# A fused attention and feed-forward kernel on one core: the first attention two steps ahead, matmuls on zeros in TensorE's waits, and batch 2 loaded ahead of two weights

## The chip, the core and the metric

The kernel runs on one core of one Trainium2 chip. The metric is the time of one execution on the device, in microseconds (us). Five engines work beside each other, each through its own list of instructions in order: TensorE (PE, matrix products and transposes), VectorE (DVE), ScalarE (ACT), GpSimd (POOL), and SyncE (SP), which here only issues transfers. POOL and SP start the transfers (DMA), and 16 DMA engines carry them out. TensorE reads SBUF and writes PSUM, from which DVE or ACT copy.

## The reference

Attention over 8 batches, 8 heads, 576 positions, 64 features a head, with 16 extra keys ("beacon") that every position sees, and after it a feed-forward part over the 4608 x 512 result:

```python
k_all = concat([beacon_k, k]); v_all = concat([beacon_v, v])
scores = q @ k_all.T / sqrt(64)           # causal over the 576, the 16 are always seen
a = softmax(scores);  attn = a @ v_all    # per batch and head
x = attn as [4608, 512]
out = ((x @ w1) * (x @ w2)) @ w3 @ w_out  # w1, w2: 512x1024, w3: 1024x1024, w_out: 1024x512
```

## The kernel before

All arithmetic of TensorE is in fp16 with sums in fp32. The work has two streams, which the program's text weaves together by hand: every engine does its instructions in the order in which the Python code issues them.

**Attention.** It goes in steps `s`, eight to a batch (`NSB`): step `s` is one half of the work for one pair of heads, `t`, of batch `b = s // 8`. `scores(s)` (L351) makes the transposed scores of the two heads in two PSUM tiles `ps`, of which there are two in all: eight matmuls in an even step, fourteen in an odd one. `exps(s, j)` (L360, ACT) writes exp of tile `j` to `pT` in SBUF and frees it. `mask(s, j)` (L372, DVE) zeroes what a position must not see. `values(s)` (L389) multiplies by the values, 6 matmuls in an even step and 24 in an odd one, into the only `psV` tile, and DVE divides by the sums into `x16` (L397, L398). The values carry a column of ones, so the sums come with them.

Scores need q and k with the features on the partitions. For batches 0 and 1 they are loaded in fp32 by SP (`load_pair`, L139), cast by DVE (`cast_pair`, L158), transposed on PE (`pe_transpose_pair`, L172) and copied out of PSUM by DVE or ACT (L178). From batch 2 on POOL's transfers load them and cast them to fp16 (`load_q`, L104, `load_k`, L113), and SP issues ten DMA transposes a batch (`transpose_qk`, L128, L129). There are two buffers for a batch's q, k and values, so batch 2 goes where batch 0 was. The last 64 rows of the fifth block of q and k are zeroed once (L481, L482).

**Feed-forward.** `emit_ff(n)` issues the next `n` matmuls of a generator, `stream()`: for blocks of 512 tokens, `ff_ab` (L279) makes (x w1) times (x w2), with ACT (L290) and DVE (L292) behind it, and `ff_out` (L300) multiplies by `Wt` and SP stores the result. `Wt` is w3 times w_out, made once by `fuse()` (L248, L257) behind the first two blocks; for this the eight pieces of w3 lie in the half of `xT` that is free so long, and w_out in `wo16`. Thirty feed-forward matmuls stand between the transposes of batch 1's q and k, 34 in steps 8 to 15, and from step 16 on about 12 in each step. x is turned into `xT` on PE for batches 0 and 1 (`pe_transpose_x`, L188), later by DMA.

**Order of the transfers.** POOL issues, one behind the other: values of batch 0, w1 and w2 (8 pieces), values of batch 1, w_out (4), w3 (8), and from step 3 on q and k of batch 2, values of batch 2, q and k of batch 3, and so on. The weights are 256 KB a piece in fp16 and are read in fp32.

The first attention is steps 0 to 7. Before the main loop stand casts and transposes of the four pairs of batch 0, with `scores(0)` and its exponentials between; in the loop each step issues the scores of the next one, and then its own values.

Of the kernel before, what the change touches and what calls it, by code (L numbers as in the profile page):

```python
# [8 lines left out]
FP32 = mybir.dt.float32  # L9
# [30 lines left out]
def kernel(  # L40
# [81 lines left out]
    def load_v(b, jt):  # L122
        load_kv(b, jt, v, beacon_v, vas[b % NB2][:, jt, :, 0:64])
# [26 lines left out]
    def cast_pair(b, t):  # L150
        if t == 0:
            b16 = bkp.tile([Nb, DM], FP16, name="b16")
            nc.vector.tensor_copy(b16, early_b[b].rearrange("p h d -> p (h d)"))
            early_b[b] = b16
        o16s[t] = []
        for i in range(2):
            o16 = tiny.tile([P, RUN, P], FP16, name=f"o16_{i}")
            nc.vector.tensor_copy(  # L158
                o16[:NR].rearrange("p j (h d) -> p h j d", h=2),
                early_qk[b, t, i][:NR].rearrange("p h (j d) -> p h j d", j=RUN),  # L160
            )
            o16s[t].append(o16)

    def pe_transpose_pair(b, t):
        qT, kT = qTs[b % NB2], kTs[b % NB2]
        for o16, dst, off, copy in (
            (o16s[t][0], qT, 0, nc.vector.tensor_copy if b or t == 0 else nc.scalar.copy),
            (o16s[t][1], kT, Nb, nc.scalar.copy),
        ):
            pt = psM.tile([P, 1024], FP16, name="pm")  # L170
            for j in range(RUN):
                nc.tensor.transpose(pt[:, ds(j * NR, NR)], o16[:NR, j, :], ident[:NR, :NR])  # L172
            if off:
                nc.tensor.transpose(
                    pt[:, ds(S, Nb)], early_b[b][:, ts(t, P)], ident[:Nb, :Nb]
                )
                copy(dst[:, t, 0:Nb], pt[:, ds(S, Nb)])
            copy(  # L178
                dst[:, t, ds(off, S)].rearrange("p (i j) -> p i j", j=RUN),
                pt[:, 0:S].rearrange("p (j i) -> p i j", j=RUN),  # L180
            )

    def pe_transpose_x(b):
        for i in range(NJT):
            pt = psM.tile([P, NT, P], FP16, name="pm")
            n = QTN[i]
            for t in range(NT):
                nc.tensor.transpose(  # L188
                    pt[:, t, 0:n], x16s[b][:n, i, ts(t, P)], ident[:n, :n]
                )  # L190
            dst = xT[:, :, ds(b * S + QT0[i], n)]
            if i % 2:
                nc.scalar.copy(dst, pt[:, :, 0:n])
            else:
                nc.vector.tensor_copy(dst, pt[:, :, 0:n])  # L195

    nc.vector.memset(ident, 1.0)
    nc.vector.memset(MA, 1.0)
# [35 lines left out]
        )  # L234
    for c in range(NJT):
        load_v(0, c)
    for c in range(4):
        for i, w in enumerate((moe_w1, moe_w2)):
            nc.gpsimd.dma_start(
                w12[:, :, ds(i * DF + c * 256, 256)],  # L240
                w[:, ts(c, 256)].rearrange("(t p) f -> p t f", p=P),
            )
# [85 lines left out]
    def emit_ff(n):  # L328
        nonlocal emitted
        for _ in range(n):  # L330
            try:
                next(ff)
            except StopIteration:
                return
            emitted += 1
# [4 lines left out]
    def scores(s):  # L340
        b, t, half = s // (2 * NT), (s // 2) % NT, s % 2
        if half == 0:
            pTs[s // 2] = ptp.tile([P, 2, PW], FP16, name="pT")
        qT, kT = qTs[b % NB2], kTs[b % NB2]
        pss[s] = []
        for g in (2 * half, 2 * half + 1):
            ps = psS.tile([P, 2, 512], FP32, name="ps")
            pss[s].append(ps)
            for jt, q0, n, col in GROUPS[g]:
                for hh in range(2):  # L350
                    nc.tensor.matmul(  # L351
                        ps[:, hh, ds(col, n)],
                        kT[ds(hh * 64, 64), t, ts(jt, P)],
                        qT[ds(hh * 64, 64), t, ds(q0, n)],
                    )

    def exps(s, j):
        g = 2 * (s % 2) + j
        pT = pTs[s // 2]
        nc.scalar.activation(  # L360
            pT[:, :, ds(GO[g], GW[g])], pss[s][j][:, :, 0 : GW[g]], AF.Exp, scale=scale
        )
# [59 lines left out]
    for s in range(2 * NSB, NS):  # L422
        fill[s] = rest * (s - 2 * NSB + 1) // n - rest * (s - 2 * NSB) // n

    cast_pair(0, 0)
    pe_transpose_pair(0, 0)
    cast_pair(0, 1)
    scores(0)
    for j in range(2):
        exps(0, j)  # L430
    pe_transpose_pair(0, 1)
    cast_pair(0, 2)
    for j in range(2):
        mask(0, j)
    pe_transpose_pair(0, 2)
    cast_pair(0, 3)
    pe_transpose_pair(0, 3)
    constants(1)
    for c in range(NJT):
        load_v(1, c)  # L440
    wo_v = moe_w_out.rearrange("(a c p) n -> a p c n", p=P, c=2)
    for a in range(4):
        nc.gpsimd.dma_start(wo16[:, ds(2 * a, 2), :], wo_v[a])
# [1 line left out]
    w316 = xT[:, :, ds(M // 2, 2 * DF)].rearrange("p a (c r) -> p a c r", c=2)  # L445
    for kt in range(NFT):
        nc.gpsimd.dma_start(w316[:, kt // 2, kt % 2], moe_w3[ts(kt, P), :])
    for s in range(NS):
        b, r = s // NSB, s % NSB
        if s == NSB - 1:  # L450
            values(s)
            pe_transpose_x(0)
            cast_pair(1, 0)
            for t in range(NT):
                emit_ff(n_first // NT)
                pe_transpose_pair(1, t)
                if t + 1 < NT:
                    cast_pair(1, t + 1)
            emit_ff(n_first - emitted)
            scores(s + 1)  # L460
            for j in range(2):
                exps(s + 1, j)
                mask(s + 1, j)
            continue
        if s + 1 < NS:
            scores(s + 1)
            exps(s + 1, 0)
        values(s)
        k1 = min(8, fill[s])
        emit_ff(k1)  # L470
        if s + 1 < NS:
            exps(s + 1, 1)
            mask(s + 1, 0)
        emit_ff(fill[s] - k1)
        if s + 1 < NS:
            mask(s + 1, 1)
        if s == 3:
            for t in range(NT):
                load_pair(1, t)
            for i in range(NB2):  # L480
                nc.vector.memset(k16s[i][64:128, 4, :], 0.0)  # L481
                nc.vector.memset(q16s[i][64:128, 4, :], 0.0)  # L482
            for c in range(NJT):
                load_q(2, c)
                load_k(2, c)
        if s == 2 * NSB - 1:
            pe_transpose_x(1)
        if 1 <= b < B - 1:
            if r == 0:
                for c in range(NJT):  # L490
                    load_v(b + 1, c)
                for c in range(NJT if b + 2 < B else 0):
                    load_q(b + 2, c)
                    load_k(b + 2, c)
            if 1 <= r <= NJT:
                transpose_qk(b + 1, r - 1)
# [31 lines left out]
```

## Time and profile before

| | us |
|---|---|
| median of three timed runs | 331.8 (330.7 to 332.42) |
| profiled execution, its own time | 331.28 |
| its span in the trace | 329.6 |
| PE busy | 296.8 (90%) |
| DVE, ACT, POOL busy | 165.4, 160.1, 107.2 |
| mean granted clock of TensorE | 0.979 of full speed |

The span runs from the first to the last instruction; the time of the execution holds some 1.7 us around it. A busy share is a mean over stages that differ. A line of the timeline gives start, duration, engine, source line, operation, output and input, their shapes and, behind an x, the number of instructions drawn together; in brackets stands the idle time ahead of the first one and what ended it. [...]

### The profile page before, as it was taken

What the parts mean: (1) busy time and instruction counts of PE and PEld (TensorE: products, weight loads), DVE (VectorE), ACT (ScalarE), POOL (GpSimd) and SP (SyncE); (2) the same over time, 40 slices, a digit from 0 to 9 for tenths busy, and PEclk for the clock granted to TensorE, in tenths of its full rate; (3) what the DMA queues carried; (4) which work ended last, traced back from release to release, by engine and by line L of the source; (5) the groups of instructions that cost most, each with busy time, mean ns of one, the idle gap of its engine ahead of it and who ended that gap; (6) DMA issues with size and microseconds to landing.
All of it is one profiled execution on the core that took longest, in us unless ns stands there. A gap on an engine that the chain in (4) does not pass through costs nothing.

```text
span 329.6 us, 6963 instructions
## 1 busy us (share of the span) xinstructions
PE 296.8 (90%) x2800; PEld 155.2 (47%) x2800; DVE 165.4 (50%) x392; ACT 160.1 (49%) x232; POOL 107.2 (33%) x143
## 2 busy tenths in 40 slices
PE   1687878727998999999999999999999999999995
PEld 1465544405444554555544555445554544444442
DVE  4546665523555544556565555555564644334442
ACT  1775366723664555356746663664666332130320
POOL 8565147757733385047408611400000000000000
PEclk9999998976999999999999999999999999999999
DMA  8999999999999299979999999991550340301103
GB/s 179 203 196 202 254 220 184 122 145 157 152 136 118 38 127 155 216 134 154 157 148 191 166 146 174 158 133 50 152 57 2 105 96 0 127 2 64 64 2 127
DMA packets 156960, 42.97 MB, mean 130 GB/s; under 512 B 143104, under 2 KB 151296, under 8 KB 156928
## 3 DMA queue, kind: packets, MB, share of 16 engines
q0 software_dynamic: 102240, 17.28, 75.2%
q1 hardware_dynamic: 54688, 25.25, 41.9%
q8 instruction: 22, 0.36, 0.4%
q14 instruction: 10, 0.08, 0.1%
HBM read 39.32 MB, written 9.44 MB: 148 GB/s over the span
## 4 chain that ended last, share of the span: by engine, by line
PE 76%; DMA 9%; ACT 5%; SPq 4%; DVE 3%; issue 1%; DVEq 0%
PE pm L279 33%; PE pm L300 19%; PE pv L389 10%; PE ps L351 8%; DMA st<-in_k_dram 7%; PE pm L257 4%; ACT pT L360 3%; DMA qT<-q 3%; ACT a_sb L290 1%; SPq L129 1%; SPq L128 1%; SPq L139 1%; PE pm L248 1%; DVE gT L292 1%; DVE o L158 1%
## 5 line engine op out<-in xcount | busy, mean ns | idle before, releaser
L279 PE MATMUL pm<-xT,w 128*128 128x512 f16 x576 | 134.3, 383 | 0.7 <-DVE xT L195 0.5
L360 ACT ACTIVATE pT<-ps 128x736 f16<-128x736 f32 (+3 forms) x128 | 106.2, 863 | 45.8 <-PE ps L351 45.3
L290 ACT ACTIVATE a_sb<-pm 128x512 f32<-128x512 f32 x72 | 43.0, 597 | 87.4 <-PE pm L279 86.4
L279 PEld LDWEIGHTS <-w 128*128 128x128 f16 x576 | 53.9, 98 | 60.5 <-issue 2.7
L292 DVE TENSOR_TENSOR gT<-pm,a_sb 128x512 f16<-128x512 f32 x72 | 49.7, 690 | 44.6 <-PE pm L279 44.2
L300 PE MATMUL pm<-Wt,gT 128*128 128x512 f16 x288 | 65.9, 379 | 0.0
L351 PE MATMUL ps<-qT,kT 64*128 64x80 f16 (+3 forms) x704 | 40.5, 243 | 14.6 <-ACT pT L360 6.0
L113 POOL DMA_DIRECT2D va<-in_v_dram x40 | 35.0, 886 | 56.7 <-PE pv L389 37.6
L389 PE MATMUL pv<-va,pT 128*128 128x65 f16 x960 | 45.2, 202 | 3.0 <-DVE x L398 1.3
L397 DVE RECIPROCAL rd<-pv 128x4 f32<-128x4 f32 x64 | 12.1, 189 | 69.9 <-PE pv L389 69.8
L389 PEld LDWEIGHTS <-pT 128*128 128x128 f16 x960 | 36.4, 102 | 14.1 <-DVE pT L372 4.3
L351 PEld LDWEIGHTS <-kT 64*128 64x128 f16 x704 | 22.3, 99 | 42.8 <-issue 31.5
L300 PEld LDWEIGHTS <-gT 128*128 128x128 f16 x288 | 27.1, 98 | 30.4
L310 DVE TENSOR_SCALAR ot<-pm 128x512 f32<-128x512 f32 x36 | 24.9, 691 | 26.0 <-PE pm L300 25.9
L398 DVE TENSOR_TENSOR x<-pv,rd 128x256 f16<-128x256 f32 x64 | 31.4, 491 | 2.3
L104 POOL DMA_DIRECT2D q<-in_q_dram x30 | 25.6, 855 | 15.9 <-DMA va<-in_v_dram 8.0
L113 POOL DMA_DIRECT2D k<-in_k_dram x30 | 25.3, 845 | 10.6 <-DMA va<-in_v_dram 7.0
L372 DVE TENSOR_TENSOR pT<-pT,MB 128x512 f16<-128x512 f16 x64 | 19.4, 324 | 0.0
L257 PE MATMUL pm<-wo,wT 128*128 128x512 f16 x64 | 16.4, 380 | 1.0 <-DVE wT L250 1.0
L172 PE MATMUL pm<-ident,o 96*128 96x96 f16 x96 | 7.8, 242 | 9.3 <-DVE o L158 8.7
L372 DVE TENSOR_TENSOR pT<-pT,MA 128x480 f16<-128x480 f16 x32 | 12.8, 399 | 1.5 <-ACT pT L360 1.5
L172 PEld LDWEIGHTS <-o 96*128 96x128 f16 x96 | 6.2, 116 | 11.6 <-DVE o L158 9.6
(40 smaller groups left out, 87.7 us busy)
## 6 DMA issues: line engine op xcount, KB each, us to landing
out_dram<-ot SPq DMA_DIRECT2D x36, 256.0 KB, 2.4
va<-in_v_dram POOLq DMA_DIRECT2D x24, 128.0 KB, 8.7
q<-in_q_dram POOLq DMA_DIRECT2D x24, 128.0 KB, 9.0
st<-in_q_dram SPq DMA_DIRECT2D x8, 288.0 KB, 7.9
st<-in_k_dram SPq DMA_DIRECT2D x8, 288.0 KB, 8.8
k<-in_k_dram POOLq DMA_DIRECT2D x18, 128.0 KB, 7.8
w<-in_moe_w_dram POOLq DMA_DIRECT2D x8, 256.0 KB, 9.8
xT<-in_moe_w_dram POOLq DMA_DIRECT2D x8, 256.0 KB, 9.8
```

Of the source, the lines that this page charges most:

```text
L104: nc.gpsimd.dma_start(q16s[b % NB2][:rows, c, :].rearrange("s (h d) -> s h d", h=H), q[b, :, ds(c * P, rows), :].rearrange("h s d -> s h d"),)
L113: nc.gpsimd.dma_start(dst[ds(p0, rows)], src[b, :, ds(s0, rows), :].rearrange("h s d -> s h d"))
L257: nc.tensor.matmul(pm, wT[:, rt, :], wo16[:, rt, :], start=(rt == 0), stop=(rt == NFT - 1),)
L279: nc.tensor.matmul(pm, w12[:, kt, ds(i * DF + kf * P, P)], xT[:, kt, ds(mc * 512, 512)], start=(kt == 0), stop=(kt == NKT - 1),)
L290: nc.scalar.activation(a_sb, pm, AF.Copy, scale=GS)
L292: nc.vector.tensor_tensor(gT[:, kf, :], pm, a_sb, ALU.mult)
L300: nc.tensor.matmul(pm, gT[:, kf, ts(mt, P)], Wt[:, kf, :], start=(kf == 0), stop=(kf == NFT - 1),)
L351: nc.tensor.matmul(ps[:, hh, ds(col, n)], kT[ds(hh * 64, 64), t, ts(jt, P)], qT[ds(hh * 64, 64), t, ds(q0, n)],)
L360: nc.scalar.activation(pT[:, :, ds(GO[g], GW[g])], pss[s][j][:, :, 0 : GW[g]], AF.Exp, scale=scale)
L372: nc.vector.tensor_tensor(blk, blk, m.unsqueeze(1).to_broadcast([P, 2, n]), ALU.mult)
L389: nc.tensor.matmul(pv[:, 2 * n + hh, 0:65], pT[:, hh, ds(col, P)], va[:, jt, 2 * t + hh, 0:65], start=(jn == 0), stop=(jn == len(BLK[i]) - 1),
L398: nc.vector.tensor_tensor(x16[:, ds(tiles[0], ni), ds(t * P, P)].rearrange("p i (h d) -> p i h d", h=2), pv[:, 0 : 2 * ni, 0:64].rearrange ...
```

## The change

Four things are changed; the arithmetic of the output stays.

1. `spin(n)` issues `n` matmuls of zeros by zeros into a PSUM tile of the feed-forward pool that nobody reads: ten ahead of everything, two ahead of `scores(0)`, two ahead of `scores(1)`, two ahead of each of the eight `values(s)` of batch 0, and two ahead of the transposes of x: 32 in all. The tile `zeros` is zeroed by DVE first of all.
2. Batch 0 has a loop of its own, in which `ahead(s + 2)` (scores and exponentials) and then `values(s)` are issued. `ahead(1)` stands between the transposes of the second and the third pair. The copies of the third and fourth q out of PSUM go from ACT to DVE. The casts of batch 1's first pair stand ahead of the transposes of x, and its loads come at step 1 in place of step 3.
3. POOL issues q, k and values of batch 2 ahead of w_out and w3.
4. The pad rows of q and k are zeroed by POOL, ahead of w1 and w2, in place of DVE at step 3.

```diff
-            (o16s[t][0], qT, 0, nc.vector.tensor_copy if b or t == 0 else nc.scalar.copy),
+            (o16s[t][0], qT, 0, nc.vector.tensor_copy if b or t != 1 else nc.scalar.copy),
...
+    zeros = const.tile([P, 512], FP16, name="zeros")
+    nc.vector.memset(zeros, 0.0)
+
+    def spin(n):
+        pm = psM.tile([P, 512], FP32, name="pm")
+        for _ in range(n):
+            nc.tensor.matmul(pm, zeros[:, 0:P], zeros)
...
     for c in range(NJT):
         load_v(0, c)
+    for i in range(NB2):
+        nc.gpsimd.memset(k16s[i][64:128, 4, :], 0.0)
+        nc.gpsimd.memset(q16s[i][64:128, 4, :], 0.0)
...
+    def ahead(s):
+        scores(s)
+        for j in range(2):
+            exps(s, j)
+
+    def masks(s):
+        for j in range(2):
+            mask(s, j)
+
+    spin(10)
     cast_pair(0, 0)
     pe_transpose_pair(0, 0)
     cast_pair(0, 1)
-    scores(0)
-    for j in range(2):
-        exps(0, j)
+    spin(2)
+    ahead(0)
     pe_transpose_pair(0, 1)
     cast_pair(0, 2)
-    for j in range(2):
-        mask(0, j)
+    masks(0)
+    spin(2)
+    ahead(1)
     pe_transpose_pair(0, 2)
     cast_pair(0, 3)
+    masks(1)
     pe_transpose_pair(0, 3)
     constants(1)
     for c in range(NJT):
         load_v(1, c)
+    for c in range(NJT):
+        load_q(2, c)
+        load_k(2, c)
+    for s in range(NSB):
+        if s + 2 < NSB:
+            ahead(s + 2)
+        spin(2)
+        values(s)
+        if s + 2 < NSB:
+            masks(s + 2)
+        if s == 1:
+            for t in range(NT):
+                load_pair(1, t)
+    for c in range(NJT):
+        load_v(2, c)
     wo_v = moe_w_out.rearrange("(a c p) n -> a p c n", p=P, c=2)
     for a in range(4):
         nc.gpsimd.dma_start(wo16[:, ds(2 * a, 2), :], wo_v[a])
...
-    for s in range(NS):
+    cast_pair(1, 0)
+    spin(2)
+    pe_transpose_x(0)
+    for t in range(NT):
+        emit_ff(n_first // NT)
+        pe_transpose_pair(1, t)
+        if t + 1 < NT:
+            cast_pair(1, t + 1)
+    emit_ff(n_first - emitted)
+    ahead(NSB)
+    masks(NSB)
+    for s in range(NSB, NS):
         b, r = s // NSB, s % NSB
-        if s == NSB - 1:
-            values(s)
-            pe_transpose_x(0)
-            cast_pair(1, 0)
...
-            continue
...
-        if s == 3:
-            for t in range(NT):
-                load_pair(1, t)
-            for i in range(NB2):
-                nc.vector.memset(k16s[i][64:128, 4, :], 0.0)
-                nc.vector.memset(q16s[i][64:128, 4, :], 0.0)
-            for c in range(NJT):
-                load_q(2, c)
-                load_k(2, c)
```

Two places of the instruction lists. POOL, from w1 and w2 on, before (`w` is w1 and w2, `va_66` and `va_67` the values of even and odd batches, `q_0` and `k_0` those of even ones, `wo` w_out, and `xT` with `in_moe_w` the place of w3):

```order
L239 DMA w_59<-in_moe_w_dram 128x4x256 x8
L113 DMA va_67<-in_v_dram 112x8x64
L117 DMA va_67<-in_beacon_v_dram 16x8x64
L113 DMA va_67<-in_v_dram 128x8x64 x3
L113 DMA va_67<-in_v_dram 80x8x64
L443 DMA wo_61<-in_moe_w_out_dram 128x2x512 x4
L447 DMA xT<-in_moe_w_dram 128x1024 x8
L104 DMA q_0_62<-in_q_dram 128x8x64
L113 DMA k_0_64<-in_k_dram 112x8x64
```

And in the changed kernel, from the last loads of q and k for batch 2 on to the first of batch 3:

```order
L104 DMA q_0_62<-in_q_dram 64x8x64
L113 DMA k_0_64<-in_k_dram 80x8x64
L113 DMA va_66<-in_v_dram 112x8x64
L117 DMA va_66<-in_beacon_v_dram 16x8x64
L113 DMA va_66<-in_v_dram 128x8x64 x3
L113 DMA va_66<-in_v_dram 80x8x64
L481 DMA wo_61<-in_moe_w_out_dram 128x2x512 x4
L485 DMA xT<-in_moe_w_dram 128x1024 x8
L104 DMA q_1_63<-in_q_dram 128x8x64
L113 DMA k_1_65<-in_k_dram 112x8x64
```

The twelve weight transfers have moved from ahead of batch 2 to behind its values.

ACT in the first attention, before, from the exponentials of step 0 to the first of step 1 (`kT_70`, `qT_68`: keys and queries of batch 0):

```order
L360 ACTIVATE pT<-ps 128x2x368
L360 ACTIVATE pT<-ps 128x2x512
L178 COPY qT_68<-pm 128x576
L177 COPY kT_70<-pm 128x16
L178 COPY kT_70<-pm 128x576
L178 COPY qT_68<-pm 128x576
L177 COPY kT_70<-pm 128x16
L178 COPY kT_70<-pm 128x576
L178 COPY qT_68<-pm 128x576
L177 COPY kT_70<-pm 128x16
L178 COPY kT_70<-pm 128x576
L360 ACTIVATE pT<-ps 128x2x384
```

And in the changed kernel, from the exponentials of step 0 to the first of step 2:

```order
L372 ACTIVATE pT<-ps 128x2x368
L372 ACTIVATE pT<-ps 128x2x512
L178 COPY qT_68<-pm 128x576
L177 COPY kT_70<-pm 128x16
L178 COPY kT_70<-pm 128x576
L372 ACTIVATE pT<-ps 128x2x384
L372 ACTIVATE pT<-ps 128x2x400
L177 COPY kT_70<-pm 128x16
L178 COPY kT_70<-pm 128x576
L177 COPY kT_70<-pm 128x16
L178 COPY kT_70<-pm 128x576
L372 ACTIVATE pT<-ps 128x2x368
```

The two exponentials of step 1 stand ahead of the key copies of the third and fourth pair, and two copies of q are gone from the list.

## Rows read from the trace of the kernel before

**Rows 1.** Busy time by stretch, all engines; behind the counts granted clock, DMA share, GB/s.

```profile
0.00:36.00 36.00, 22.66 (x280) 16.64 (x280) 18.34 (x65) 19.79 (x30) 22.22 (x35) 1.00 1.43 199
...
67.30:75.50 8.20, 0.49 (x4) 0.13 (x4) 0.89 (x3) 0.78 (x1) 4.97 (x7) 0.65 1.80 147
75.50:81.40 5.90, 5.60 (x53) 3.53 (x53) 2.36 (x6) 2.11 (x4) 4.21 (x6) 0.62 2.12 155
...
103.00:329.00 226.00, 220.53 (x1941) 110.05 (x1940) 113.75 (x248) 103.48 (x146) 45.59 (x57) 1.00 0.92 109
```

**Rows 2.** Timeline of PE from 66 to 86 us.

```profile
66.26 1.03 PE L279 MATMUL pm<-xT,w 128*128 128x512 f16 x4
...
75.51 0.61 PE L351 MATMUL ps<-qT,kT 64*128 64x256 f16 x4 [4.48 <-DMA qT<-q]
...
81.43 0.52 PE L351 MATMUL ps<-qT,kT 64*128 64x128 f16 x14
81.88 0.35 PE L389 MATMUL pv<-va,pT 128*128 128x65 f16 x6
...
85.24 0.90 PE L389 MATMUL pv<-va,pT 128*128 128x65 f16 x24
```

**Rows 3.** Timeline of POOL: a selection, then issues of transfers.

```profile
1.15 0.29 POOL L211 TENSOR_SCALAR_AFFINE_SELECT ident<-ident 128x128 f16<-128x128 f16 x1 [0.63 <-DVE ident L197]
...
14.79 1.60 POOL L239 DMA_DIRECT2D w<-in_moe_w_dram  x2 [2.25 <-DMA va<-in_v_dram]
...
40.53 0.53 POOL L447 DMA_DIRECT2D xT<-in_moe_w_dram  x1 [5.90 <-DMA va<-in_v_dram]
...
46.35 0.53 POOL L447 DMA_DIRECT2D xT<-in_moe_w_dram  x1 [0.75 <-DMA wo<-in_moe_w_out_dram]
48.30 0.90 POOL L104 DMA_DIRECT2D q<-in_q_dram  x1 [1.42 <-DMA xT<-in_moe_w_dram]
...
65.73 0.73 POOL L113 DMA_DIRECT2D va<-in_v_dram  x1 [2.05 <-DMA k<-in_k_dram]
```

**Rows 4.** Timeline of PE in the first 51 us.

```profile
6.73 1.14 PE L172 MATMUL pm<-ident,o 96*128 96x96 f16 x12 [6.73 <-DVE o L158]
...
18.47 1.50 PE L389 MATMUL pv<-va,pT 128*128 128x65 f16 x24
19.91 0.83 PE L351 MATMUL ps<-qT,kT 64*128 64x128 f16 x14
...
21.62 1.03 PE L351 MATMUL ps<-qT,kT 64*128 64x128 f16 x8
...
31.59 1.72 PE L389 MATMUL pv<-va,pT 128*128 128x65 f16 x24 [0.74 <-DVE x L398]
...
50.02 1.90 PE L279 MATMUL pm<-xT,w 128*128 128x512 f16 x4
```

**Rows 5.** Timeline of ACT, behind the last transposes of batch 0.

```profile
15.79 0.65 ACT L178 COPY kT<-pm 128x576 f16<-128x576 f16 x1
16.32 3.28 ACT L360 ACTIVATE pT<-ps 128x768 f16<-128x768 f32 x4
```

**Rows 6.** Transfers by line: operation, count, KB each, median us from issue to landing.

```profile
xT<-in_moe_w_dram POOLq DMA_DIRECT2D x8, 256.0 KB, 9.8
```

**Rows 7.** Timeline of PE, the fused weights and scores(25).

```profile
102.39 0.61 PE L248 MATMUL pm<-ident,xT 128*128 128x128 f16 x8
...
115.81 0.52 PE L351 MATMUL ps<-qT,kT 64*128 64x128 f16 x14
```

**Rows 8.** Timeline of SP, the last transpose of batch 3.

```profile
91.77 1.26 SPq L129 DMA_TRANSPOSE kT<-k  x1
```

**Rows 9.** That transpose by its source line.

```profile
DMA to landing us min/median/max: 8.3/8.3/8.3
```

**Rows 10.** Timeline of DVE, a cast of the fourth pair.

```profile
14.29 0.56 DVE L158 CAST o<-st 96x768 f16<-96x768 f32 x1 [0.71 <-DMA st<-in_k_dram]
```

More of the change, by code (lines that the diff above doesn't have):

```diff
@@ L447 @@
         nc.gpsimd.dma_start(w316[:, kt // 2, kt % 2], moe_w3[ts(kt, P), :])
-    for s in range(NS):
-        b, r = s // NSB, s % NSB
-        if s == NSB - 1:
-            values(s)
-            pe_transpose_x(0)
-            cast_pair(1, 0)
-            for t in range(NT):
[L455 to L463, printed above, removed]
-            continue
+    cast_pair(1, 0)
[10 more added lines that the diff above has]
+    for s in range(NSB, NS):
+        b, r = s // NSB, s % NSB
         if s + 1 < NS:
@@ L476 @@
             mask(s + 1, 1)
-        if s == 3:
-            for t in range(NT):
-                load_pair(1, t)
-            for i in range(NB2):
-                nc.vector.memset(k16s[i][64:128, 4, :], 0.0)
-                nc.vector.memset(q16s[i][64:128, 4, :], 0.0)
-            for c in range(NJT):
-                load_q(2, c)
-                load_k(2, c)
         if s == 2 * NSB - 1:
@@ L489 @@
             if r == 0:
-                for c in range(NJT):
+                for c in range(NJT if b > 1 else 0):
                     load_v(b + 1, c)
```

## Prediction

> **What bounds the kernel now.** I read the busy time by stretch first. From 103 us to the end TensorE (PE) is busy for 220.53 of 226 us at the full clock [rows 1]. What PE gets rid of before that moves everything behind it forward, to the end. Ahead of it there are two losses. Between 67.3 and 75.5 us PE is busy for 0.49 us, and from 75.5 to 81.4 us its granted clock is 0.62; and in the first 36 us it is busy for 22.66 us only [rows 1].
>
> The timeline of PE says what it waits for at 67 us. Its last block of feed-forward matmuls ends at 66.26 + 1.03 = 67.29; then the second half of scores(16), the first scores of batch 2, waits for transposed queries until 75.51 [rows 2]. The POOL queue shows why these came late: the transpose needs the loaded rows, and the loads of q for batch 2 start at 48.30, behind all pieces of w_out and w3, of which the last six go out between 40.53 and 46.35, each held until an older transfer has landed [rows 3]. So the stall is a matter of order in a full queue.
>
> In the first attention the clock column reads 1.00 [rows 1], but 24 value matmuls take 1.50 us at 18.47 and 0.90 us at 85.24, and fourteen score matmuls 0.83 us at 19.91 and 0.52 us at 81.43 [rows 2, 4]. [...] ScalarE (ACT) ends the last key copy at 15.79 + 0.65 = 16.44 and then has 14 exponentials left, seven steps, the first four of them in 3.28 us, 0.82 us each [rows 5]. Fed without a gap it would be done at 27.9, but the values of the last step run until 31.59 + 1.72 = 33.3 [rows 4]. What is lost there is PE at the low level and neighbouring steps that wait for each other.
>
> **The change part by part.**
>
> *Loads of batch 2 ahead of w_out and w3.* Twelve transfers of 256 KB leave their place ahead of q and k. The last of them went out every (46.35 - 40.53) / 5 = 1.16 us [rows 3], so q and k of batch 2 come about 12 x 1.16 = 14 us earlier, and so do the ten DMA transposes, which wait on SP for nothing else: the one that released PE at 75.5 would land near 61.5. PE asks for it at 67.3 less the gain of the first attention (2.3 us, below), at 65.0. That leaves 3.5 us, and the stall goes. PE then does at the full clock what it did from 75.51 to the scores at 81.43 [rows 2], the rest of step 15 and the transposes of x for batch 1. That took 5.9 us at a granted 0.62; all scaled it is 3.7, not scaled 5.9; since copies out of PSUM lie between the transposes I take 4.6. Scores(17) then start at 67.3 + 4.6 = 71.9 instead of 81.43: 9.5 us (8.2 to 10.4).
>
> What is late next? First w3. It now stands behind q, k and v of batch 2, which took POOL from 48.30 to 65.73, and the end of its transfer moves from 46.35 + 9.8 = 56 by as much, to about 75, or 80 with the transposes beside it [rows 3, 6]. The fused weights start at 102.39 [rows 7], which becomes 90.6: 10 us to spare. The load of v for batch 2 stands ahead of the weights in POOL and waits for values(7), done by 31 us, before POOL gets there. Second, batch 3: its q and k have the same bytes ahead of them as before, so their last transpose still leaves SP at 91.77 and lands 8.3 us later, at 100.1 [rows 8, 9]; scores(25), at 115.81 before [rows 7], need it and now come at 104.0. That is 4 us to spare, and 115.8 - 100.1 = 15.7 us is the most that the whole change can give.
>
> [...]
>
> *The first attention.* Scores(s+2) now stand ahead of values(s), in place of scores(s+1), and the scores and exponentials of step 1 lie in the wait for the pairs of q and k. When the last key copy is done ACT has six steps left in place of seven. VectorE (DVE) copies the third and fourth q in place of ACT, and the third copy stands ahead of the fourth pair's casts (0.56 us each, [rows 10]), so that it and not the loads sets the last pair; I give it the 0.65 us of such a copy on ACT [rows 5]. ACT's floor is 16.44 + 0.65 + 12 x 0.82 = 26.9. A pair of steps costs PE at the full clock 0.52 each for its two sets of scores (the eight of the first at half of 1.03), 0.35 + 0.90 for values, and 1.03 for four matmuls on zeros, as for the four of that shape at 66.26 [rows 2, 4]: 3.3 us, as much as four exponentials on ACT, so the two keep pace. The second half of the last scores, 0.35 us, starts with two exponentials to go, at 25.3; behind it come 2.15 us of values (steps 5 to 7), six zeros (1.55) and about 0.5 for the one PSUM buffer of the values: the last values end at 29.8, 3.5 us before 33.3. At the low level a pair costs 1.03 + 0.83 + 1.50 [rows 4], about 0.58 for the six values (scaled as the 24) and 4 x 0.475 for the zeros (four of the shape take 1.90 us at 50.02) [rows 4]: 5.8 us; three pairs from 16.4 and the last two steps (4.0) end at 37.9: 4.6 us later than before. No row of before has matmuls on zeros, so both ends stand. I take a gain of 2.3: ahead of the rises near 36 and 80 us PE ran values, transposes and feed-forward matmuls close together, and the zeros make this stretch alike; but a first part at the low level is likely.
>
> The ten zeros ahead of all (4.75 us at the low level) end before the first transposes at 6.73 [rows 4], and the four in the next two waits before ACT's key copies are done: free, 1 us at the most if they run past them. The casts for batch 1 are now made ahead of the copies of x, 1.1 us of DVE [rows 10] on the way to the first feed-forward matmul, against about as much that the transposes of x gain at the full clock: zero, give or take 1.
>
> [...]
>
> *Pad rows on POOL.* Four fills of 64x512, ahead of w1 and w2. A selection over 128 columns takes 0.29 us there [rows 3]; four times the columns 1.2, all four 4.6 at the most, and 0.4 at the least. The weights queue behind v, for which POOL stood still for 2.25 us ahead of 14.79 [rows 3], and what the fills delay is issued into a queue that is still full: free; uncovered, 4.6. Four fills leave DVE, where PE did not wait for them. The loads of q and k for batch 1 move from step 3 to step 1, about 4 us earlier, and meet w1 and w2 in place of v; nothing waits for them for long before: zero.
>
> The sum, against the profiled execution's own 331.28 us (span 329.6; 0.5 us under the median of 331.8): 331.3 - 9.5 - 2.3 = 319.5.
>
> **The rivals.**
>
> *The zeros never raise the clock* in the first attention: it loses 4.6 us, the rest wins 9.5: 326.4. For it: PE ran 16 to 33 us at the low level, with small gaps. Against: gaps like the 0.74 us ahead of 31.59 [rows 4] are what the zeros fill. 0.15.
>
> *The clock is up from the first scores on*, and the transposes of x win their 1 us too: 3.5 to 4.5 us and 9.5 to 10.4, with the ceiling 315.6 to 318. 0.20.
>
> *A part of the stall stays.* The loads of batch 1 come earlier too and share the engines, so not all of the 14 us are handed on: with the transpose at 66 to 72 there are 1 to 7 us of stall and some of the low clock, 321 to 328. 0.12.
>
> *The wait is only renamed.* [...] 0.04.
>
> *The weights become the late transfer* (the slower side). Place: the first transposes of w3, at 90.6 by my sum. Each microsecond by which w3's first rows land after that is one of PE; from 102.4 on the change is slower, and at 106 it costs 4 us, 335. For it: the DMA engines are full (their share is above 1 in the first 36 us and from 67 to 81 us [rows 1]). Against: they move the same bytes in another order, and the first w3 would have to land some 30 us after the 71 or so that I expect. 0.05.
>
> **How the numbers follow.** My forecast has the remaining 0.44, 317.5 to 322. About 0.5% is what a timing of this kernel can tell from no change; all but the last two rivals are faster by more: 0.91. The renamed wait is the same, 0.04; the late weights are slower, 0.05. For 8 in 10 I go from the ceiling, 315.5, to 327, which takes in the cold case and most of the part stall.
>
> **What would show it.** The wait of scores(16) for the transposes is gone or under 1 us, and no stretch near 75 us has a granted clock of 0.6. The 24 value matmuls take 0.9 us from some point between 12 and 22 us on; if they take 1.5 us to the end of the first attention, the zeros failed. Scores(17) come near 69.6, the fused weights near 90.6 without a wait for w3, scores(25) near 104. I am wrong if PE waits there for a weight, or if the stall has a new releaser and the old length.

## The result, and the profile of the changed kernel

| | before | after |
|---|---|---|
| median | 331.41 us (330.7 to 332.42, 4 runs) | 321.12 us (320.11 to 321.72, 4 runs) |
| profiled execution, span | 331.28, 329.6 | 321.72, 319.7 |
| PE busy | 296.8 (90%) | 299.1 (94%) |

The ratio is 0.9684 (95% interval 0.9645 to 0.9723): 10.3 us faster. Two later measurements of the same kernel, each beside runs of the one before, gave 0.9714 (0.9678 to 0.975) and 0.9746 (0.9722 to 0.977). The forecast was 319.5, in a range of 315.5 to 327. In two of the kernels measured further on a few executions are over 1.5% longer than that kernel's fastest; medians hold them, ratios leave them out.

Line numbers have moved: L204 are the zeros, L363 the scores, L372 the exponentials, L401 the values, L188 the transposes of x, L291 and L312 the feed-forward matmuls, L260 the transposes of w3. First the busy time by stretch (columns as in [rows 1]: start and end, length, PE, PEld, DVE, ACT and POOL busy, granted clock as a share of full speed, DMA share, GB/s).

```profile
0.00:36.00 36.00, 28.48 (x318) 16.46 (x319) 20.85 (x66) 18.56 (x29) 23.75 (x37) 0.81 1.34 212
...
67.30:75.50 8.20, 7.71 (x110) 4.94 (x111) 4.65 (x14) 6.05 (x10) 4.61 (x7) 1.00 1.17 207
75.50:92.00 16.50, 15.79 (x164) 7.97 (x161) 8.86 (x22) 10.58 (x16) 12.96 (x17) 1.00 2.14 140
93.00:319.00 226.00, 220.69 (x1940) 110.06 (x1940) 113.21 (x247) 103.61 (x146) 51.20 (x64) 1.00 1.06 116
```

The stretch of 67.3 to 75.5 us holds 7.71 us of PE's work in place of 0.49, and the granted clock is 1.00 behind it, where it was 0.62 [rows 1]. The last 226 us are as full as before, 220.69 against 220.53, and start 10 us earlier. PE is busy for 5.8 us more in the first 36, but the profile's page puts 12.0 us on the 32 zeros: the busy share is no measure of what was won. The same place in PE's timeline, for [rows 2]:

```profile
65.53 1.03 PE L291 MATMUL pm<-xT,w 128*128 128x512 f16 x4
66.49 0.55 PE L363 MATMUL ps<-qT,kT 64*128 64x128 f16 x8
...
70.13 0.92 PE L188 MATMUL pm<-ident,x 128*128 128x128 f16 x12 [0.43 <-DVE gT L304]
70.98 0.52 PE L363 MATMUL ps<-qT,kT 64*128 64x128 f16 x14
```

Scores(16) run all eight matmuls without a wait, and scores(17) start at 70.98 in place of 81.43: 10.45 us. From scores(16) to scores(17) it takes 4.49 us. In the kernel before, both halves of scores(16) had waited, the first four matmuls for the transposed keys and the other four, from 75.51 [rows 2], for the queries:

```profile
70.55 0.49 PE L351 MATMUL ps<-qT,kT 64*128 64x128 f16 x4 [3.25 <-DMA kT<-k]
```

POOL shows the cause, and the pad rows ahead of it, for [rows 3]:

```profile
8.36 0.81 POOL L247 MEMSET k<- 64x512 f16 x1
9.11 0.93 POOL L248 MEMSET q<- 64x512 f16 x1
...
26.12 0.88 POOL L104 DMA_DIRECT2D q<-in_q_dram  x1 [0.32 <-DMA w<-in_moe_w_dram]
...
50.34 0.70 POOL L481 DMA_DIRECT2D wo<-in_moe_w_out_dram  x1
...
68.06 0.53 POOL L485 DMA_DIRECT2D xT<-in_moe_w_dram  x1 [0.49 <-DMA wo<-in_moe_w_out_dram]
69.31 0.89 POOL L104 DMA_DIRECT2D q<-in_q_dram  x1 [0.73 <-DMA xT<-in_moe_w_dram]
```

The first q of batch 2 is issued at 26.12 in place of 48.30, the last piece of w3 at 68.06 in place of 46.35. The first attention on PE, for [rows 4]:

```profile
1.27 3.64 PE L204 MATMUL pm<-zeros 128*128 128x512 f16 x10 [1.27 <-DVE zeros L199]
6.70 0.98 PE L172 MATMUL pm<-ident,o 96*128 96x96 f16 x12 [1.79 <-DVE o L158]
...
19.75 1.47 PE L401 MATMUL pv<-va,pT 128*128 128x65 f16 x24
...
24.01 0.89 PE L401 MATMUL pv<-va,pT 128*128 128x65 f16 x24
...
30.55 0.90 PE L401 MATMUL pv<-va,pT 128*128 128x65 f16 x24 [0.30 <-DVE x L410]
...
34.76 1.46 PE L291 MATMUL pm<-xT,w 128*128 128x512 f16 x6 [0.42 <-DVE xT L195]
```

The ten zeros end before the first transposes, which start when they did before. The 24 values take 1.47 us at 19.75 and 0.89 at 24.01: the granted clock reads 0.50 from 8 to 21 us and 1.00 from there to 36 us. These two are the low and the high level of this text; by them the 24 values of 1.50 us in [rows 4] ran at the low one, although the reading of [rows 1] is 1.00 there. The last values end at 31.45 (33.31 before), the first feed-forward matmul starts at 34.76 (36.15). What stands further on, for [rows 7]:

```profile
91.95 0.61 PE L260 MATMUL pm<-ident,xT 128*128 128x128 f16 x8
...
105.36 0.52 PE L363 MATMUL ps<-qT,kT 64*128 64x128 f16 x14
...
133.30 0.40 PE L363 MATMUL ps<-qT,kT 64*128 64x256 f16 x4 [0.41 <-DMA qT<-q]
```

The fused weights start without a wait for w3, 10.44 us earlier, and scores(25) 10.45 us earlier. Scores(32), the first of batch 4, now wait for a transpose; no such wait stood there before. From scores(25) to scores(33) 0.6 us are lost (10.45 us earlier, then 9.86), the last loss on the way: 9.9 us reach the end of the span.

### The profile page after: what moved, and what is told of

Same layout as the page of the kernel before. It is cut to its first block, busy times and chain, and to the rows that moved or that the text cites. A ratio compares the mean times of both kernels' runs of the same rounds, so it can differ in the third digit from the quotient of the medians.

```text
span 319.7 us, 7027 instructions
## 1 busy us (share of the span) xinstructions
PE 299.1 (94%) x2832; PEld 153.5 (48%) x2832; DVE 167.3 (52%) x391; ACT 158.8 (50%) x230; POOL 109.9 (34%) x147
## 4 chain that ended last, share of the span: by engine, by line
PE 79%; ACT 7%; DVE 5%; DMA 5%; issue 2%; SPq 1%; DVEq 0%
PE pm L291 34%; PE pm L312 18%; PE pv L401 11%; PE ps L363 8%; PE pm L269 5%; ACT pT L372 4%; DMA st<-in_k_dram 3%; DMA qT<-q 2%; ACT a_sb L302 2%; DVE gT L304 2%; DVE o L158 1%; PE pm L204 1%; PE pm L260 1%; SPq L139 1%; PE pm L172 1%
## 5 line engine op out<-in xcount | busy, mean ns | idle before, releaser
L291 PE MATMUL pm<-xT,w 128*128 128x512 f16 x576 | 133.2, 381 | 0.6 <-DVE xT L195 0.4
L372 ACT ACTIVATE pT<-ps 128x736 f16<-128x736 f32 (+3 forms) x128 | 106.1, 863 | 41.2 <-PE ps L363 40.7
L291 PEld LDWEIGHTS <-w 128*128 128x128 f16 x576 | 53.7, 98 | 59.9 <-issue 1.7
L312 PE MATMUL pm<-Wt,gT 128*128 128x512 f16 x288 | 65.9, 379 | 0.0
L363 PE MATMUL ps<-qT,kT 64*128 64x80 f16 (+3 forms) x704 | 38.6, 236 | 7.1 <-ACT pT L372 6.5
L401 PE MATMUL pv<-va,pT 128*128 128x65 f16 x960 | 42.0, 196 | 1.2 <-DVE x L410 0.8
L312 PEld LDWEIGHTS <-gT 128*128 128x128 f16 x288 | 27.1, 98 | 30.4
L401 PEld LDWEIGHTS <-pT 128*128 128x128 f16 x960 | 34.3, 99 | 12.8 <-issue 4.0
L363 PEld LDWEIGHTS <-kT 64*128 64x128 f16 x704 | 21.7, 97 | 35.9 <-issue 33.6
L204 PE MATMUL pm<-zeros 128*128 128x512 f16 x32 | 12.0, 490 | 1.3 <-DVE zeros L199 1.3
## 6 DMA issues: line engine op xcount, KB each, us to landing
xT<-in_moe_w_dram POOLq DMA_DIRECT2D x8, 256.0 KB, 11.4
```

The source lines that it names most:

```text
L291: nc.tensor.matmul(pm, w12[:, kt, ds(i * DF + kf * P, P)], xT[:, kt, ds(mc * 512, 512)], start=(kt == 0), stop=(kt == NKT - 1),)
L312: nc.tensor.matmul(pm, gT[:, kf, ts(mt, P)], Wt[:, kf, :], start=(kf == 0), stop=(kf == NFT - 1),)
L363: nc.tensor.matmul(ps[:, hh, ds(col, n)], kT[ds(hh * 64, 64), t, ts(jt, P)], qT[ds(hh * 64, 64), t, ds(q0, n)],)
L372: nc.scalar.activation(pT[:, :, ds(GO[g], GW[g])], pss[s][j][:, :, 0 : GW[g]], AF.Exp, scale=scale)
L401: nc.tensor.matmul(pv[:, 2 * n + hh, 0:65], pT[:, hh, ds(col, P)], va[:, jt, 2 * t + hh, 0:65], start=(jn == 0), stop=(jn == len(BLK[i]) - 1),
```

## The experiments

The places in a line of the table come from one profile, and so from one execution; median and ratio come from several, the ratio against runs of the kernel before on the same chip. The columns give the end of values(7) and the starts of scores from PE's timeline, in us. The profiled execution can lie apart from the median, by 2.5 us in "after, second time" (323.81 against 321.35), so differences of 1 to 2 us between the places of two lines decide nothing.

| run | values(7) end | scores(8) | (17) | (25) | (33) | median | ratio, 95% interval |
|---|---|---|---|---|---|---|---|
| before | 33.31 | 47.13 | 81.43 | 115.81 | 147.13 | 331.41 | |
| after | 31.45 | 46.56 | 70.98 | 105.36 | 137.27 | 321.12 | 0.9684 [0.9645, 0.9723] |
| loads only | 32.13 | 45.91 | 69.30 | 109.27 | 141.53 | 324.32 | 0.9771 [0.9726, 0.9816] |
| attention only | 29.78 | 44.12 | 77.61 | 111.98 | 143.29 | 330.09 | 0.999 [0.9971, 1.0008] |
| no zeros | 31.47 | 49.38 | 73.77 | 108.14 | 139.46 | 323.53 | 0.9775 [0.9744, 0.9806] |
| pads on DVE | 30.19 | 45.96 | 70.46 | 104.84 | 138.93 | 322.02 | 0.9745 [0.9708, 0.9783] |
| after, second time | 30.37 | 46.96 | 70.35 | 104.73 | 138.50 | 321.35 | 0.9714 [0.9678, 0.975] |
| more zeros | 29.67 | 44.56 | 67.95 | 102.33 | 136.54 | 322.92 | 0.9773 [0.9741, 0.9805] |
| casts after x | 29.76 | 43.36 | 66.75 | 101.39 | 137.19 | 321.66 | 0.9719 [0.9698, 0.974] |
| transposes earlier | 30.16 | 45.45 | 68.85 | 103.22 | 135.69 | 321.07 | 0.9708 [0.968, 0.9736] |
| after, third time | 29.99 | 45.29 | 68.68 | 103.07 | 136.92 | 321.97 | 0.9746 [0.9722, 0.977] |
| transposes dense | 30.78 | 46.07 | 69.46 | 103.83 | 139.69 | 324.56 | 0.9828 [0.98, 0.9856] |
| dense, casts after x | 29.63 | 43.26 | 67.85 | 102.22 | 137.06 | 322.72 | 0.9772 [0.9739, 0.9805] |
| dense, casts, more zeros | 30.10 | 43.86 | 67.26 | 102.87 | 141.44 | 325.19 | 0.9828 [0.9806, 0.9851] |

The profile of "loads only" is of an execution of 326.0 us, above the median; its early places are used, its end is not.

### Each half alone

The kernel before, with the loads alone in the new order (and the pad rows zeroed by DVE at the start, since they must be zero before those loads); the cut is shortened:

```diff
-        if s == 3: ... load_q(2, c); load_k(2, c)      # behind w_out and w3
+    for c in range(NJT): load_q(2, c); load_k(2, c)    # ahead of the loop
+        if s == NSB - 1: load_v(2, ...); w_out; w3
```

> The kernel before with the order of POOL's loads alone changed (q, k and values of batch 2 ahead of w_out and w3; pad rows zeroed by DVE at the start, which that needs); the first attention as before, without zeros. Theory: the stall at 67 us is a matter of that order alone. Scores(16) then start at about 67.3 without a wait, scores(17) at about 71.8 in place of 81.4: a gain of 9.7 us, about 321.7 us. Rival: the loads come early enough only together with the earlier loads of batch 1 that the new first attention brings, and 2 to 5 us of the wait stay: 324 to 327. Second rival: DVE's casts get slower beside POOL's issues of q and k and the transposes of batch 1 come 0.8 us later: 322.5.

The ratio of 0.9771 is 7.6 us of gain (6.1 to 9.1 by its interval), from the order of the transfers alone: most of the whole. The stall at scores(16) is gone, but in the profiled execution a shorter wait stands at scores(17):

```profile
72.85 0.52 PE L354 MATMUL ps<-qT,kT 64*128 64x80 f16 x10 [3.21 <-DMA kT<-k]
```

The last key transpose of batch 2 went out at 56.08, among the weights, and landed 16.7 us later. Behind the wait the granted clock is 0.55 from 73 to 78 us; with both, scores(18) follow scores(17) after 8.9 us, 3.3 in the changed kernel. Whether other executions of this kernel wait there, no trace shows.

And the changed kernel with w_out and w3 back ahead of batch 2 (shortened):

```diff
-    load_q(2, ...), load_k(2, ...) ... load_v(2, ...); w_out; w3
+    w_out; w3 ... load_q(2, ...), load_k(2, ...); load_v(2, ...)
```

> The changed kernel with w_out and w3 ahead of q, k and values of batch 2 again; the new first attention, zeros and pads on POOL stay. Theory: scores(16) wait for the transposes as before, near 75 us, and whatever the first attention gains (1.9 us at its end) is lost in that wait: 331 to 331.8, no change. Rival: the two parts add up, 329.5 or less. In the same profile DVE's casts for batch 1 take 0.55 us each if POOL's issues of q and k slowed them in the changed kernel, and 0.8 to 0.9 us if it was something else.

No change, 0.999, although in the profile the first attention did its part: scores(8) come at 44.12, 3.0 us earlier. PE takes this gain to scores(16) and waits there:

```profile
67.92 0.49 PE L363 MATMUL ps<-qT,kT 64*128 64x128 f16 x4 [4.83 <-DMA kT<-k]
72.29 0.61 PE L363 MATMUL ps<-qT,kT 64*128 64x256 f16 x4 [3.89 <-DMA qT<-q]
72.83 1.50 PE L401 MATMUL pv<-va,pT 128*128 128x65 f16 x24
```

The wait is 8.7 us, against 7.7 before, and the values behind it run at the low level, 1.50 us. That the stall swallows the gain rests on the median, not on this profile: it is of the fastest of twelve executions, 328.4 us against a median of 330.09, the last wait in it ends 3.2 us earlier than in the profile before (72.29 against 75.51), and scores(17) come 3.8 us earlier. By themselves the halves are worth 7.6 and 0.3 us, together 8.4 to 10.4 in the three measurements. What remains, 0.5 to 2.5 us, would be what the stall had swallowed of the first attention, but the interval of the first half alone is as wide: that the halves give more together than apart is not shown.

### The zeros

`spin` does nothing (the tile of zeros goes too):

```diff
-            nc.tensor.matmul(pm, zeros[:, 0:P], zeros)
+            return
```

> The changed kernel without any matmul on zeros; all else stays. Theory: the zeros raise the clock near 21 us; without them the first attention runs at the low level to its end, a pair of steps costs PE 3.9 us in place of 3.3 on ACT, the last values end at 33 in place of 31.4 us, and the whole is 1 to 1.6 us slower than the changed kernel: 322.2 to 322.8. Rival: the zeros only take PE's time, the last values end at the same time or earlier without them: 320.5 to 321.2.

PE's timeline of this kernel, the last values and what follows:

```profile
29.97 1.50 PE L397 MATMUL pv<-va,pT 128*128 128x65 f16 x24 [0.73 <-DVE x L406]
...
35.05 1.44 PE L287 MATMUL pm<-xT,w 128*128 128x512 f16 x3 [0.41 <-DVE xT L195]
35.43 2.76 PE L287 MATMUL pm<-xT,w 128*128 128x512 f16 x6
```

All values run at the low level, the sets of 24 in 1.50 us, and yet the last end at 31.47, as in the first profile of the changed kernel. Two steps ahead, without zeros, is enough for these 1.8 us: while the level is low, two zeros cost about 1 us of PE in each step (1.04 us at 16.84 in the changed kernel). In the nine other profiles with zeros and both halves the last values ended at 29.6 to 30.8, so there the zeros won 0.7 to 1.8 us up to this place; in one of them, the changed kernel's second, 24 values already take 0.89 us at 19.24. They pay more behind it. Six feed-forward matmuls take 2.76 us here at 35.43, at the low level, 1.46 in the changed kernel, and scores(8) come at 49.38, 2.8 us later. By the ratios the zeros are worth 0.3 to 0.9% (0.9775 against 0.9684, 0.9714 and 0.9746), less than the profiles suggest, and only the first of the three lies clear of it: the intervals of the other two overlap with its own.

More zeros (16 at the start, four in each of the next waits, four ahead of the last pair's transposes):

```diff
-    spin(10)
+    spin(16)
... (the other places left out)
```

> The changed kernel with 16 zeros in place of 10 at the start, 4 in place of 2 ahead of scores(0) and scores(1), and 4 ahead of the transposes of the fourth pair. Theory: the first zeros raise the clock at 4 us and the gap up to the first transposes lets it fall; with the gaps filled it stays, step 0's values run at the high level, and the first attention ends at 29.7 in place of 31.4 us: 0.5 to 1.7 us faster than the changed kernel. Rival: where the rise comes later, the added zeros run at the low level (0.43 us each) and stand in the path: 0.5 to 2 us slower.

By the durations the clock is up from the first scores on (eight take 0.55 us at 8.90, 0.92 in the changed kernel), the granted clock reads 1.00 from there to the end of batch 1 (0.998 as the mean of the whole execution), and scores(17) come at 67.95, 3 us before those of the changed kernel's first profile. The time is 322.92, not better than the 321.35 beside it. So a whole first attention at the full clock, the rival in which the clock is up from the first scores on, was reached, and it gave nothing that the times show: between scores(17) and scores(33) 2.3 of the 3 us went.

### The pad rows, and the casts of batch 1

The pad rows zeroed by DVE at the start, in place of POOL (one of the two lines):

```diff
-        nc.gpsimd.memset(k16s[i][64:128, 4, :], 0.0)
+        nc.vector.memset(k16s[i][64:128, 4, :], 0.0)
```

> The changed kernel with the pad rows zeroed by DVE at the start in place of POOL. Theory: the four fills on POOL were hidden behind the transfer of the values: same time as the changed kernel within 0.4 us, 320.8 to 321.5. Rival: POOL's fills slowed DVE's casts beside them (0.87, 0.95 and 0.65 us in place of 0.55), and without them the first attention is 0.3 to 0.6 us earlier: 320.5.

0.9745 lies within what the changed kernel itself gave on three occasions: the pads' place is worth nothing that can be measured. The four fills take about 3 us of POOL.

The casts of batch 1's first pair behind the transposes of x and their copies:

```diff
-    cast_pair(1, 0)
     spin(2)
     pe_transpose_x(0)
+    cast_pair(1, 0)
```

> The changed kernel with the casts of batch 1's first pair behind the copies of x again. Theory: they stood in the path to the first feed-forward matmul, 3.3 us from the last values to it in three profiles against 2.2 us in the profile of the loads alone, at the same clock: the first feed-forward matmul comes 1.1 us earlier, 2.2 us behind the last values, and the whole is 0.5 to 1.1 us faster. Rival: the first transposes of batch 1 then wait for the casts and the 1.1 us come back: no change at scores(8).

The first feed-forward matmul stands 2.34 us behind the last values (32.10 less 29.76), against 3.3 in the changed kernel: the casts ahead of the copies of x cost 1.0 us. The time does not follow, 321.66. PE has scores(17) 4.2 us earlier than in the first profile of the changed kernel (3.6 and 1.9 us than in the others) and gives it back here:

```profile
131.53 0.39 PE L363 MATMUL ps<-qT,kT 64*128 64x256 f16 x4 [2.60 <-DMA qT<-q]
```

Behind this wait the granted clock is 0.72 from 131 to 137 us, and scores(33) come at 137.19.

One more loss lies in the same stage. DVE's casts of batch 1's first and last pair, in the first profile of the changed kernel:

```profile
32.53 1.01 DVE L158 CAST o<-st 96x768 f16<-96x768 f32 x2
...
43.35 1.56 DVE L158 CAST o<-st 96x768 f16<-96x768 f32 x2
```

Two casts take 1.01 us while POOL waits and 1.56 us while it issues loads of q and k without a pause (40.10 to 44.5). In the kernel before POOL was at the weights then. From the first feed-forward matmul to scores(8) it takes 11.8 us in place of 11.0, and 11.0 again in "attention only" (44.12 less 33.09), where the loads of q are not there and the casts of the last pair take 1.06 us. In the changed kernel a single one of batch 1's eight casts takes 0.54 to 0.92 us, 0.55 in the median; why the casts grow beside POOL's issues, no run shows.

### What is late next

The changed kernel again, beside "casts after x" and the next one, and later beside the last three:

> The changed kernel itself, beside the three that follow, so that they are compared on one chip. All theories: 0.965 to 0.975 of the kernel before, and a first attention that ends between 29.7 and 31.5 us, by when the clock rises in the run that is profiled.

> The changed kernel once more, beside the three that follow on the same chip. Both theories: 321 to 322 us, scores(32) waits 0.4 to 2.5 us for a DMA transpose of batch 4.

Scores(33) come at 138.50 and 136.92, with waits of 2.27 and 1.67 us at scores(32) for queries: the wait of 0.41 in the first profile is longer in the others. In SP's queue the transposes of batch 4 stand among the output stores (the changed kernel's first profile):

```profile
109.32 1.19 SPq L129 DMA_TRANSPOSE kT<-k  x1
118.50 0.38 SPq L323 DMA_DIRECT2D out_dram<-ot  x1
118.97 1.21 SPq L128 DMA_TRANSPOSE qT<-q  x1
...
130.94 1.18 SPq L128 DMA_TRANSPOSE qT<-q  x1
```

Between the first pair and the second, SP stands for 8 us, since the first store waits for its tile; the last q of batch 4 goes out at 130.94, and scores(32) want it at 132.9. So the transposes were issued one step earlier:

```diff
-            if 1 <= r <= NJT:
-                transpose_qk(b + 1, r - 1)
+            if 0 <= r < NJT:
+                transpose_qk(b + 1, r)
```

> The changed kernel with each batch's DMA transposes issued one step earlier (steps 0 to 4 of the batch ahead in place of 1 to 5), so ahead of one more step's output transfers in SP's queue. Theory: scores(32) waited 0.4 us for a transposed q in the profile of the changed kernel and 2.4 us in that of the pads on DVE, since SP's transposes stand behind output transfers; issued earlier the wait is gone: 0.6 to 2.6 us faster. Rival: the loads of q and k, not SP's order, set those transposes; the wait stays and the time is the same.

The wait for the transpose is gone; a shorter one, for DVE's mask, stands in its place, and the median, 321.07 against 321.35, has not moved:

```profile
130.42 0.55 PE L363 MATMUL ps<-qT,kT 64*128 64x128 f16 x8
130.90 0.24 PE L401 MATMUL pv<-va,pT 128*128 128x65 f16 x2
131.73 0.54 PE L401 MATMUL pv<-va,pT 128*128 128x65 f16 x12 [0.59 <-DVE pT L384]
```

Then all ten in the first three steps, and with it the casts behind x, and with both more zeros:

```diff
-            if 1 <= r <= NJT:
-                transpose_qk(b + 1, r - 1)
+            for c in ((0, 1), (2, 3), (4,))[r] if r < 3 else ():
+                transpose_qk(b + 1, c)
```

> The changed kernel with the ten DMA transposes of a batch issued in the first three steps of the batch ahead of it (chunks 0 and 1, 2 and 3, 4) in place of one chunk in each of the steps 1 to 5. Theory A (SP's order): batch 4's transposes stand on SP among the output stores, the first of which waits 8 us for its tile, so that the last transpose leaves at 131 to 132 us however early PE comes; issued ahead of the first store they leave by about 117, scores(32) waits for no DMA, and scores(33) follows scores(25) after 31.3 us as in the kernel before (115.81 to 147.13). That gives back the 0.6 to 2.5 us lost there: 319 to 321 us, 0.3 to 0.8% under the changed kernel. Theory B (the transfer engines are full): the transposes land no earlier, the wait stays, 321 to 322 us.

> As the one before, and the casts of batch 1's first pair behind the copies of x as in the kernel before the change, which alone won 3.6 us at scores(17) in one profile and gave it back at scores(32). Theory A: what the first attention wins is kept: scores(33) at 133 to 135 us in place of 137, 317 to 319 us. Theory B: 321 to 322 us, scores(33) at 136.5 or later.

> As the one before, with 16 zeros at the start, four ahead of scores(0) and scores(1) and four more ahead of the last pair's transposes, so that the granted clock is high from the start and no later fall is left to chance. Theory A: 316.5 to 318.5 us, at most 1 us under the one before; scores(33) at 133 to 134.5. Theory B: 321 to 322 us. A third way, batch 3's transposes late behind w3: scores(24) or scores(25) waits for a DMA near 98 to 102 us and the gain ends there.

On the same chip the changed kernel has 321.97. Two of the three are slower, 324.56 and 325.19; the second, 322.72, is not told apart from it. Theory A is wrong in its end: the wait for the transposes is gone, as it said, but scores(33) follow scores(25) after 35.9 us, not 31.3. PE and DVE of "transposes dense", one after the other:

```profile
127.34 0.48 PE L401 MATMUL pv<-va,pT 128*128 128x65 f16 x10 [2.78 <-DVE pT L384]
```

```profile
126.44 0.69 DVE L322 TENSOR_SCALAR ot<-pm 128x512 f32<-128x512 f32 x1 [3.56 <-DMA out_dram<-ot]
127.05 0.23 DVE L384 TENSOR_TENSOR pT<-pT,MB 128x160 f16<-128x160 f16 x1
...
130.85 0.69 DVE L322 TENSOR_SCALAR ot<-pm 128x512 f32<-128x512 f32 x1 [2.20 <-DMA out_dram<-ot]
```

DVE stands with an output tile until an older store has landed, and the mask that PE needs stands behind it on DVE. In the two other runs PE waits 3.4 and 4.4 us for masks. The stores are late since the transposes of batch 4 now go first: the first store goes out at 119.74, 15.9 us behind scores(25), against 13.1 in the changed kernel (118.50). Theory B is wrong in its letter (the wait did not stay) and closer in its sense. The landing times of the output stores between 100 and 150 us, before, in the third profile of the changed kernel, and in "transposes dense":

```profile
DMA to landing us min/median/max: 2.3/3.9/5.3
```

```profile
DMA to landing us min/median/max: 3.5/6.7/8.3
```

```profile
DMA to landing us min/median/max: 2.3/6.3/7.8
```

And the stretch from 100 to 118 us in the changed kernel (columns as above):

```profile
100.00:118.00 18.00, 18.00 (x202) 9.74 (x199) 7.99 (x20) 10.32 (x15) 11.98 (x16) 1.00 2.26 150
```

PE did the same work before from 110.45 to 128.45, and there the DMA share was 1.50, at 111 GB/s; now it is 2.26, at 150 (the share counts the time of packets, and passes 1 here). POOL shows where the difference comes from. In the kernel before it had issued the last load of batch 4's q and k at 101.18 and stood until PE was done with older values:

```profile
112.82 0.82 POOL L113 DMA_DIRECT2D va<-in_v_dram  x1 [10.91 <-PE pv L389]
```

In the changed kernel the same last load goes out at 101.86, no earlier, while PE is 10.45 us ahead, and the loads of batch 4's values follow at once, at 102.57. The 10.9 us that POOL had to spare are used up. In the eleven profiles with both halves of the change, scores(17) lie between 66.75 and 73.77, and scores(33) between 135.69 and 141.44, in no order that follows the first. Shown is that the stretch before batch 4 takes back what comes early, by the transpose in one order and by the store in the other. That the cause is the transfers' rate and not one more queue fits the landing times and POOL's lost pause; no run took bytes away there, so this stays open.

## Why the prediction was right, and where it was not

*The stall.* Right in mechanism and nearly in size. From the end of the feed-forward block to scores(17) it was to take 4.6 us, and it took 4.42 (70.98 less 66.56). The prediction passed over the first half of scores(16), which waited until 70.55 for its keys; that costs it nothing, since these landed early too. The loads come even earlier than the 14 us forecast: the first q goes out 22 us earlier, since the first of the twelve weights took POOL longer than the 1.16 us by which all were counted (it stood 5.90 us ahead of 40.53 alone [rows 3]). The fourth q transpose, the one that had released PE at 75.5, went out at 50.15 and landed at 57.5 (61.5 in the prediction). No part of the stall stayed, and the order of the loads alone, 7.6 us, bears the most of it.

*The renamed wait.* The last key transpose of batch 2 went out at 54.32, when all of w_out had been issued, and took as long as this to land, against 6.5 to 7.3 us for the key transposes from 42 to 50 us:

```profile
DMA to landing us min/median/max: 11.4/11.4/11.4
```

So a transpose issued beside the weights took longer; what makes it so, no run shows. It landed at 65.75, and scores(17) want it at 70.98: the late transpose of the rival with 0.04 is there, but not the wait, with 5 us to spare. In the profile of "loads only" the same transpose took 16.7 us and did hold PE, for 3.2 us: the margin is not large.

*The weights.* w3 landed from 69.0 to 78.3 (71 and 75 to 80 in the prediction), the fused weights started at 91.95 (90.6) without a wait. That rival did not come about.

*The first attention, the term that was mis-sized.* 2.3 us were forecast, 0.7 arrived at the feed-forward block ahead of scores(16) in the first profile (66.26 less 65.53); the later profiles of the same kernel had 1.4 and 3.0, so the size hangs on the execution that is profiled. The last values won 1.9 us (33.31 less 31.45), and two things took 1.3 back before scores(8). The casts ahead of the copies of x ("zero, give or take 1") cost 1.0 by the experiment, of which half came back, with the transposes of x at the full clock (the first twelve in 0.84 us, 1.42 before): from the last values to the first feed-forward matmul it takes 3.3 us in place of 2.84. And the stage of batch 1's pairs takes 0.8 more, with DVE's casts beside POOL's issues, which the sum did not have. The clock rose at 21 us, within the forecast's "between 12 and 22"; but in "no zeros" the last values ended as early with no rise at all. So the gain of this stretch in the first profile does not come from the zeros: the new order without them wins as much at the low level, and the zeros pay above all in the stage behind it. The rival without a rise was not met: the clock rose at 21 us in the first profile, and before 19.24 us in the second, where 24 values take 0.89 us.

*What was costed at nothing.* The zeros at the start, the pads and the earlier loads of batch 1 cost nothing that shows in the traces; only the pads were taken out by themselves.

*The ceiling.* The step that failed is "what is late next". It looked at w3 and batch 3, found 4 us to spare at batch 3, which held (no wait at scores(24) or (25) in the changed kernel), and put the ceiling at 15.7 us from there. It did not ask the same of batch 4, whose last q lands just as scores(32) want it: [rows 7] ended at scores(25). The best of all runs has scores(33) 11.4 us earlier (147.13 less 135.69), so the rival at 315.6 to 318 was out of reach in every order tried. In the profiled execution the sum comes out so: of the 11.8 us forecast 1.6 are missing in the first attention, 0.6 go at scores(32) and 0.3 outside the span (2.0 us in place of 1.7), and the stall gave 0.2 more; that leaves 9.5, against 331.28 less 321.72 = 9.56.

## What to carry to other kernels

A wait that is taken away from a pipeline of equal stages can come back some stages on, here two batches later: work out the landing time of every later batch, not of the next one, before a gain is called free. A gain ahead of a stall can be lost in the stall, so a part is judged in the company it will have. A single profile is one execution: before a place in it is explained, it is held against the median and a second profile of the same kernel. And an instruction queue that holds transposes and stores moved the wait with every new order here; where no order helps, the transfers' total is the next thing to look at.

## What was not expected of the hardware

In the changed kernel three of the four fills of 64x512 in fp16 take 0.81 to 0.93 us on GpSimd, the last 0.52; a selection of 128 columns takes 0.29 [rows 3]. Beside GpSimd's issues of loads, a pair of VectorE's casts took 1.56 us, at 43.35, in place of 1.01, at 32.53. The time at which TensorE's clock rises in the first attention differs from run to run of one kernel: it rose at 21 us in the first profile of the changed kernel, and in the second the 24 values at 19.24 already took 0.89 us, so differences of 1 to 2 us in a single profile of this stage say little.
